# An attention and mixture-of-experts kernel on one core: five steps of blocks 2 to 4 change places in the order table

## The chip, the cores and the metric

The kernel runs on one core of a Trainium2 chip. The metric is device time in microseconds (us), the median of the runs; lower is better. The core's engines work side by side, each through its own instructions in a fixed order: TensorE (PE; PEld is its weight load), VectorE (DVE), ScalarE (ACT), GpSimd (POOL) and SyncE (SP), which issues most transfers.

## The reference

A gated linear attention runs over 768 steps for 4 x 8 heads of width 48; its output, laid out as 3072 tokens of 384 numbers, goes through a three-way maximum layer and then through a layer that sends each token to one of 8 experts.

```python
for t in range(S):
    state = alpha[:, :, t, :, None] * state + np.einsum('bhd,bhe->bhde', k[:, :, t], v[:, :, t])
    y[:, :, t] = np.einsum('bhd,bhde->bhe', q[:, :, t], state)
...
h = np.maximum(np.maximum(x @ w1, x @ w2), x @ w3)
return (h @ w_out).astype(np.float32)
...
e_idx = np.argmax(logits, axis=1)
...
h = np.maximum(x[mask] @ w1[e], 0.0)
ye = h @ w2[e]
out[mask] = gate_w[mask, None] * eom[mask, e, None] * ye
```

## The kernel before, in words

The 3072 tokens are eight blocks of 384, numbered 0 to 7. Blocks 2b and 2b+1 are the two halves of batch b. Each block passes through these steps:

- **Preparation of q and k** (DVE). `prep_z` runs a scan backwards over the decay factors into a tile `Z` (L196), `prep_k` multiplies k by it (L201), `prep_p` forms inverses and runs a forward scan over the same tile (L208 to L211), `prep_q` multiplies q by that (L215). Each is done once for either half b of the head pairs. There is one `Z`, so the four steps of one half end before those of the next begin. `check` and `check_pl` (ACT, L180 and L182) test the factors' range.
- **Attention by chunks.** `last` calls `attend`, which finishes one chunk (c, b) and begins the next: on PE transposes (L307), products with the state (L298), with the scores (L314) and with v (L320), new scores (L327); on DVE the state (L341, L343) and the masked scores A (L354); on ACT the state's decay (L346) and a copy of the result into `x32` (L351). The result of a block's last chunk is the last part of its x.
- **Split.** `split_x` cuts x into a high part (ACT, L368) and a low part (DVE, L369), three pieces each.
- **First layer.** `mm1` is called 18 times for a block (6 slices f, 3 matrices w). A call is a group of nine matmuls (L457) into one of three PSUM banks of the pool psM. ACT copies the group of w = 0 (`hm`, L461); DVE takes the maximum with those of w = 1 (L464) and w = 2 (L467); ACT and POOL then split the result (L478, L483). A bank is free again when it has been read.
- **Second layer.** `mm2` multiplies a tile of 128 tokens into `ops` (L493), and ACT copies the logits and the row out (L499, L500).
- **Routing** of a block. `route_a` finds the expert of each token and the running counts, eleven small DVE instructions (L528 to L544) with two exponentials on ACT (L532, L546); `route_b` forms ranks on PE (L551, L552, tile `rps`); `route_c` works the ranks out on DVE, beginning with the read of `rps` at L564; `route_d` forms the weights (L586 to L594).

For blocks 2 and up `ops` lies in the pool psO, and so does `rps` of `route_b` for all blocks but the last. That pool has one buffer, so the next user waits until the last reader of the one before is done:

```python
psO = pool("psO", bufs=1, space=PSUM)
...
free = i == NBLK - 1 and t == 1 or not general and (i == 0 or i == 1 and t != 1)
ops[t] = bank(psM, "M", "ops") if free else bank(psO, "O", "ops")
...
ps = rtmp["ps"] = bank(psO, "O", "rps") if i < NBLK - 1 else bank(C["psR"], "R", "rps")
```

The order of the work is a table written by hand. `on(t, f, ...)` notes a step with a place number t, `seq(t, dt, ...)` a row of steps that are dt apart; the steps are sorted by t and called in that order, and each engine works its instructions off in the order in which they were called. Numbers matter only by comparison: `mm1(i, f, w)` of blocks 2 and up has the number 18i + 3f + w, `mm2(2, 0)` has 54.9. The steps of the change have numbers between 30 and 54.

Of the kernel before, what the change touches and what calls it, by code (L numbers as in the profile page):

```python
# [88 lines left out]
def layers(tc, pool, wk, K, general, *args):  # L89
    with ExitStack() as ctx:  # L90
        _layers(ctx, tc, pool, wk, K, general, *args)


def _layers(ctx, tc, pool_, wk, K, general, qk, al, a0, v, vT, w123, wout, gates, ew1, ew2, out):
# [263 lines left out]
    def finish_x(i):  # L358
        for c in range(3):
            for h in range(2):  # L360
                (nc.sync if i < 2 else nc.scalar).dma_start(out=x32[i][64 * h + D:64 * h + 64, c],
                                                            in_=x32[i][64 * h + 16 * c:64 * h + 16 * c + 16, 3])
# [765 lines left out]
    def on(t, f, *a):  # L1128
        ev.append((t, len(ev), f, a))

    def seq(t, dt, *steps):

        for n, (f, *a) in enumerate(steps):
            on(t + n * dt, f, *a)
# [4 lines left out]
    if not general:  # L1139
        batches = [(c, b) for c in range(CPB) for b in (1, 0)]  # L1140

        def last(i, x, y=None):

            def f():
                attend(x and (i, *x), y and (i, *y))
                if x == (2, 1):
                    finish_x(i)
            return (f,)
# [57 lines left out]
        for (i, f), x in zip(order, steps):  # L1206
# [5 lines left out]
        lo, hi = range(3), range(3, 6)  # L1212
# [4 lines left out]
            (mm2, 0, 2, hi), (load_qkv, 3), (mm2, 1, 0, lo), last(2, (2, 1), (0, 0)), (check, 2, 0, 0),  # L1217
            (mm2, 1, 0, hi), (mm2, 1, 1, lo), last(2, (0, 0), (1, 0)), (check, 2, 0, 1), (load_a, 3, 0),
            (prep_z, 3, 1), (mm2, 1, 1, hi), last(2, (1, 0), (2, 0)), (prep_k, 3, 1),
            (mm2, 1, 2, lo), (check_pl, 3), (prep_p, 3, 1), last(2, (2, 0)), (split_x, 2), (mm2, 1, 2, hi), (prep_q, 3, 1),  # L1220
            (route_a, 0))
        seq(37.3, 0.9, (prep_z, 3, 0), (check, 3, 1, 0), (prep_k, 3, 0), (check, 3, 1, 1), (prep_p, 3, 0), (check, 3, 0, 0),
            (prep_q, 3, 0), (check, 3, 0, 1))
        seq(49.7, 0.6, (route_b, 0), (route_c, 0), (route_d, 0), (route_a, 1))
        seq(52.7, 0.6, (route_b, 1), (route_c, 1), (route_d, 1))
        on(42.9, load_a, 4, 1)
        on(45.1, load_a, 4, 0)

# [261 lines left out]
```

## Time and profile before

| what | value |
|---|---|
| median of 3 runs | 734.69 us (733.62 to 734.71) |
| the profiled execution's own time | 733.51 us |
| its span | 731.8 us |
| PE busy, share of the span | 699.3 us, 96% |
| DVE, ACT, POOL busy | 399.7, 290.3, 125.8 us |
| mean granted TensorE clock | 0.988 |

The span runs from the first to the last instruction. All starts below are microseconds from the span's start. An engine's idle time stands in square brackets before the instruction that ended it, with what released it. PEclk 1.00 is the clock's upper level (2.4 GHz), 0.50 the lower one (1.2 GHz). The changed steps lie between 147 and 211 us; blocks 2 to 7, and behind them the experts, follow.

### The profile page before, as it was taken

The numbers are of one execution on the slowest core, as the hardware profiler recorded it, in microseconds if no ns is written. First come the engines' busy times: TensorE is split into PE (matmuls) and PEld (weight loads), VectorE is DVE, ScalarE is ACT, GpSimd is POOL, SyncE is SP. The second block draws the span as 40 slices with busy tenths as digits, with TensorE's granted clock in tenths as the row PEclk, the third lists the DMA queues.
The fourth block names the chain that finished last, engine by engine and source line by source line (L and its number), as shares of the span: only waits on it lengthen the run. The fifth ranks groups of instructions, "written<-read, shape, count | busy, mean of one in ns | idle before, by whom it ended". The sixth has DMA issues, their size and how long they took to land.

```text
span 731.8 us, 14142 instructions
## 1 busy us (share of the span) xinstructions
PE 699.3 (96%) x5103; PEld 657.4 (90%) x5103; DVE 399.7 (55%) x951; ACT 290.3 (40%) x761; POOL 125.8 (17%) x136
## 2 busy tenths in 40 slices
PE   8999999999899999999999999989999999999992
PEld 7888999889799999998999999989879899999992
DVE  6868887376876736736324255664125254225451
ACT  4345533545543533524323214323224354334451
POOL 1000000001111111211111114042223233332320
PEclk9999999999999999999999999999999999999997
DMA  9906310651231510400000015016547342125430
GB/s 252 366 19 188 105 46 2 179 150 43 72 95 36 136 41 20 128 22 21 2 33 9 12 33 226 23 43 224 207 165 266 127 143 60 57 79 187 141 114 21
DMA packets 23069, 74.91 MB, mean 102 GB/s; under 512 B 7962, under 2 KB 12132, under 8 KB 19888
## 3 DMA queue, kind: packets, MB, share of 16 engines
q1 hardware_dynamic: 17424, 60.95, 25.4%
q0 software_dynamic: 4384, 11.72, 5.2%
q10 hardware_dynamic: 1152, 0.89, 0.5%
q8 instruction: 56, 0.92, 0.5%
q14 instruction: 53, 0.43, 0.2%
HBM read 100.67 MB, written 9.94 MB: 151 GB/s over the span
## 4 chain that ended last, share of the span: by engine, by line
PE 78%; DVE 9%; issue 4%; ACT 3%; DMA 3%; ACTq 1%; POOL 0%; SPq 0%; DVEq 0%; POOLq 0%
PE hps L457 25%; PE psM L990 13%; PE psP L1047 12%; PE ops L493 9%; PE sc L327 4%; PE y L314 3%; DMA out<-yo,sidx 2%; PE y L298 2%; PE psw L1122 1%; PE psM L982 1%; PE psP L982 1%; DVE Z L211 1%; PE XT L307 1%; PE psH L951 1%; DVE wu L414 1%
## 5 line engine op out<-in xcount | busy, mean ns | idle before, releaser
L990 PE MATMUL psM<-cx,w1H 128*128 128x256 f32 (+1 forms) x576 | 110.3, 290 | 3.2 <-DVE ch L997 3.2
L483 POOL TENSOR_TENSOR hL<-hm,hH 128x384 fp32r<-128x384 f32 x36 | 42.2, 1172 | 399.1 <-ACT hH L478 399.1
L457 PE MATMUL hps<-xH,wH 128*128 128x384 f32 x432 | 104.6, 349 | 1.5 <-ACT xH L368 1.3
L457 PE MATMUL hps<-xH,wL 128*128 128x384 f32 x432 | 99.1, 337 | 1.6 <-DVE wL L426 1.6
L1047 PE MATMUL psP<-w2H,ch 128*128 128x384 f32 x368 | 99.3, 341 | 1.0 <-issue 1.0
L457 PE MATMUL hps<-xL,wH 128*128 128x384 f32 x432 | 99.0, 336 | 0.0
L990 PEld LDWEIGHTS psM<-cx,w1H 128*128 128x128 f32 x576 | 90.9, 188 | 4.5 <-DVE ch L997 4.1
L997 DVE SCALAR_TENSOR_TENSOR ch<-psM,ch 128x256 fp32r<-128x256 f32 (+1 forms) x128 | 43.8, 371 | 91.0 <-ACT ch L994 83.4
L990 PE MATMUL psM<-cx,w1L 128*128 128x256 f32 (+1 forms) x288 | 83.2, 289 | 0.0
L457 PEld LDWEIGHTS hps<-xH,wH 128*128 128x128 f32 x432 | 74.7, 189 | 7.4 <-ACT xH L368 2.1
L457 PEld LDWEIGHTS hps<-xH,wL 128*128 128x128 f32 x432 | 77.4, 189 | 2.3 <-DVE wL L426 2.3
L457 PEld LDWEIGHTS hps<-xL,wH 128*128 128x128 f32 x432 | 77.7, 189 | 0.2 <-DVE xL L369 0.2
L1047 PEld LDWEIGHTS psP<-w2H,ch 128*128 128x128 f32 x368 | 66.8, 188 | 3.8 <-issue 3.1
L493 PE MATMUL ops<-wo,hH 128*128 128x400 f32 x258 | 68.4, 346 | 0.2
L464 DVE TENSOR_TENSOR hm<-hm,hps 128x384 f32<-128x384 f32 x48 | 26.4, 551 | 70.6 <-PE hps L457 65.1
L994 ACT ACTIVATE ch<-psM 128x256 fp32r<-128x256 f32 (+1 forms) x96 | 37.9, 401 | 61.0 <-PE psM L990 58.4
L1047 PE MATMUL psP<-w2L,ch 128*128 128x384 f32 x184 | 61.7, 335 | 0.1
L990 PEld LDWEIGHTS psM<-cx,w1L 128*128 128x128 f32 x288 | 54.5, 189 | 0.0
L478 ACT CAST hH<-hm 128x384 fp32r<-128x384 f32 x43 | 22.0, 512 | 81.6 <-DVE hm L467 77.8
L1010 POOL DMA_INDIRECT out<-yo,sidx x27 | 28.9, 1072 | 128.7 <-ACT yo L1058 30.2
L493 PEld LDWEIGHTS ops<-wo,hH 128*128 128x128 f32 x258 | 47.0, 188 | 1.3 <-ACT hH L478 0.5
L493 PE MATMUL ops<-wo,hL 128*128 128x400 f32 x129 | 44.5, 345 | 0.5 <-POOL hL L483 0.5
(263 smaller groups left out, 1122.1 us busy)
## 6 DMA issues: line engine op xcount, KB each, us to landing
s1a<-in_ew SPq DMA_DIRECT2D x12, 1536.0 KB
s2a<-in_ew SPq DMA_DIRECT2D x12, 1536.0 KB
s1b<-in_ew SPq DMA_DIRECT2D x8, 1536.0 KB
s2b<-in_ew SPq DMA_DIRECT2D x8, 1536.0 KB
ws<-in_w SPq DMA_DIRECT2D x6, 1152.0 KB
at<-in_al SPq DMA_DIRECT2D x16, 336.9 KB
vt<-in_v SPq DMA_DIRECT2D x8, 576.0 KB
x2d<-xs SPq DMA_DIRECT2D x24, 192.0 KB
```

Of the source, the lines that this page charges most:

```text
L314: mm(y[64 * h:64 * h + D, g], vt[i][:, c, hh * D:(hh + 1) * D], A[:, h, g], start=(first and g == 0 and not on_pe), stop=True, skip_group_ ...
L327: mm(sc[:, h, g * L:(g + 1) * L], kt[ni][r, 2 * nb + g, ncs], qt[ni][r, 2 * nb + g, ncs], start=True, stop=True)
L457: mm(ps, slab(a, f)[:, w, k], b[i][:, k], start=(n == 0), stop=(n == 8))
L464: nc.vector.tensor_max(m, m, ps)
L478: nc.scalar.copy(hH[i, f], m)
L483: (nc.gpsimd if not general and i > 1 else nc.vector).tensor_sub(hL[i, f], hps["m"], hH[i, f].bitcast(F32))
L493: mm(ps[:, :DM + NG], a[i, f][:, ts_], wo[f // 3][:, b, f % 3], start=(f + n == 0), stop=(f + n == 7))
L990: mm(ps, w[:, k, f * 128:(f + 1) * 128], x[:, k, :n], start=(k + m == 0), stop=(k + m == 4))
L994: nc.scalar.activation(chid(0, f, slice(0, n)), ps, AF.Relu)
L997: nc.vector.scalar_tensor_tensor(C["h"][f // 4][:, f % 4, to:to + b - a], ps[:, a:b], 0.0, chid(0, f, slice(a, b)).bitcast(F32), op0=ALU.m ...
L1010: nc.gpsimd.indirect_dma_start(out=out[:, :], out_offset=bass.IndirectOffsetOnAxis(ap=sidx[:p, c:c + 1], axis=0), in_=y[:p], in_offset=Non ...
L1047: mm(ps[:, :DM], chid(x, f, slice(128 * t, 128 * t + 128)), w[:, f], start=(f + n == 0), stop=(f == NE - 1 and n == 2))
```

## The change

Only the table's numbers and the places of steps in it change; every instruction is kept.

```diff
@@ -1217,12 +1217,13 @@
             (mm2, 0, 2, hi), (load_qkv, 3), (mm2, 1, 0, lo), last(2, (2, 1), (0, 0)), (check, 2, 0, 0),
             (mm2, 1, 0, hi), (mm2, 1, 1, lo), last(2, (0, 0), (1, 0)), (check, 2, 0, 1), (load_a, 3, 0),
             (prep_z, 3, 1), (mm2, 1, 1, hi), last(2, (1, 0), (2, 0)), (prep_k, 3, 1),
-            (mm2, 1, 2, lo), (check_pl, 3), (prep_p, 3, 1), last(2, (2, 0)), (split_x, 2), (mm2, 1, 2, hi), (prep_q, 3, 1),
+            (mm2, 1, 2, lo), (check_pl, 3), last(2, (2, 0)), (split_x, 2), (mm2, 1, 2, hi), (prep_p, 3, 1), (prep_q, 3, 1),
             (route_a, 0))
         seq(37.3, 0.9, (prep_z, 3, 0), (check, 3, 1, 0), (prep_k, 3, 0), (check, 3, 1, 1), (prep_p, 3, 0), (check, 3, 0, 0),
-            (prep_q, 3, 0), (check, 3, 0, 1))
-        seq(49.7, 0.6, (route_b, 0), (route_c, 0), (route_d, 0), (route_a, 1))
-        seq(52.7, 0.6, (route_b, 1), (route_c, 1), (route_d, 1))
+            (check, 3, 0, 1), (prep_q, 3, 0))
+        seq(49.7, 0.6, (route_b, 0), (route_c, 0), (route_d, 0))
+        on(51.9, route_a, 1)
+        seq(53.2, 0.4, (route_b, 1), (route_c, 1), (route_d, 1))
         on(42.9, load_a, 4, 1)
         on(45.1, load_a, 4, 0)
 
```

`prep_p(3, 1)` moves behind the last chunk of block 2, `split_x(2)` and `mm2(1, 2, hi)`. `prep_q(3, 0)` and `check(3, 0, 1)` change places. `route_a(1)` moves from 51.5 to 51.9, `route_b(1)` from 52.7 to 53.2, `route_c(1)` from 53.3 to 53.6 and `route_d(1)` from 53.9 to 54.0.

On DVE, at the split of block 2's x (Z, d and pl belong to the preparation of block 3, xL is the split's low part):

```order
 L201 TENSOR_TENSOR kt<-kt,Z 112x768
+L343 TENSOR_TENSOR state<-state,y 48x2x48 x2
+L369 TENSOR_TENSOR xL<-x_1347,xH 128x384 x3
 L208 TENSOR_SCALAR d_131<-Z 112x2x3
 L209 TENSOR_TENSOR pl<-pl,Z 112x6
 L210 RECIPROCAL d_131<-d_131 112x2x3
 L211 SCALAR_TENSOR_TENSOR Z<-at,d_131 112x769
-L343 TENSOR_TENSOR state<-state,y 48x2x48 x2
-L369 TENSOR_TENSOR xL<-x_1347,xH 128x384 x3
 L215 TENSOR_TENSOR qt<-qt,Z 112x768
```

The last state and the split's subtractions stand ahead of the inverses and the forward scan of the preparation now; the multiplication of q stays behind both.

On DVE, at block 1's routing, the changed order from the last instruction of `route_a(1)` to the first two of `route_c(1)` (L564 reads `rps`; Z and kt belong to block 5, state and A to block 4):

```order
+L544 TENSOR_REDUCE z<-rv 128x3
+L369 TENSOR_TENSOR xL<-x_1825,xH 128x384 x3
+L464 TENSOR_TENSOR hm<-hm,hps 128x384
+L467 TENSOR_TENSOR hm<-hm,hps 128x384
+L196 SCALAR_TENSOR_TENSOR Z<-at,dz 112x769
+L201 TENSOR_TENSOR kt<-kt,Z 112x768
+L341 COPY state<-y 48x2x48 x2
+L354 TENSOR_TENSOR A<-sc,mask 128x512
 L564 TENSOR_TENSOR rd<-rps,oh 128x24
 L568 TENSOR_REDUCE ri<-rd 128x3
```

The scan, the product with k, the state and the mask (L196, L201, L341, L354) stand ahead of L564 now; they stood behind `route_c(1)`. The whole of `route_a(1)` also moved behind the preparation L208 to L215 of block 4, ahead of which it stood.

On PE, at the same place (hps is the last group of nine of block 2, `mm1(2, 5, 2)`; XT begins a chunk of block 4):

```order
+L457 MATMUL hps<-xH,wH_885 128x384 x3
+L457 MATMUL hps<-xL,wH_885 128x384 x3
+L457 MATMUL hps<-xH,wL_886 128x384 x3
 L551 LDWEIGHTS ut
 L551 MATMUL rps<-oh,ut 128x24
 L552 LDWEIGHTS ones
 L552 MATMUL rps<-oc,ones 128x24
-L457 MATMUL hps<-xH,wH_885 128x384 x3
-L457 MATMUL hps<-xL,wH_885 128x384 x3
-L457 MATMUL hps<-xH,wL_886 128x384 x3
 L307 MATMUL XT<-ident,kt 128x112 x2
```

The two matmuls into `rps` moved behind one group of nine and stand directly ahead of the chunk. POOL's and SP's orders are the same as before.

## Rows read from the trace of the kernel before

**Rows 1.** The page: busy time of each engine, then the chain that ended last.

```profile
PE 699.3 (96%) x5103; PEld 657.4 (90%) x5103; DVE 399.7 (55%) x951; ACT 290.3 (40%) x761; POOL 125.8 (17%) x136
...
PE 78%; DVE 9%; issue 4%; ACT 3%; DMA 3%; ACTq 1%; POOL 0%; SPq 0%; DVEq 0%; POOLq 0%
```

**Rows 2.** Timeline, PE waits: start us, us, engine line op out<-in, [idle before <- releaser].

```profile
152.51 1.27 PE L457 MATMUL hps<-xH,wH 128*128 128x384 f32 x3 [1.33 <-ACT xH L368]
...
197.39 0.19 PE L551 MATMUL rps<-oh,ut 128*128 128x24 bf16 x1 [0.71 <-DVE oh L538]
...
201.47 0.71 PE L327 MATMUL sc<-qt,kt 48*128 48x128 f32 x8 [0.89 <-DVE qt L215]
```

**Rows 3.** Timeline around the split of block 2's x, DVE, ACT and PE.

```profile
149.00 0.35 PE L320 MATMUL y<-vt,kn 128*48 128x48 f32 x8
...
150.59 0.49 DVE L343 TENSOR_TENSOR state<-state,y 48x96 f32<-48x96 f32 x2
...
151.95 1.34 ACT L368 CAST xH<-x 128x384 fp32r<-128x384 f32 x3
...
152.49 1.49 DVE L369 TENSOR_TENSOR xL<-x,xH 128x384 fp32r<-128x384 f32 x3 [1.41 <-ACT xH L368]
...
156.60 0.18 DVE L544 TENSOR_REDUCE z<-rv 128x3 f32<-128x24 f32 x1
...
156.93 0.46 ACT L461 COPY hm<-hps 128x384 f32<-128x384 f32 x1
...
158.17 0.56 DVE L464 TENSOR_TENSOR hm<-hm,hps 128x384 f32<-128x384 f32 x1 [1.39 <-PE hps L457]
```

**Rows 4.** Timeline, PE: starts of block 2's first groups, and the transpose after six.

```profile
154.98 1.17 PE L457 MATMUL hps<-xH,wH 128*128 128x384 f32 x3
...
157.86 0.80 PE L457 MATMUL hps<-xH,wH 128*128 128x384 f32 x3
...
159.53 0.68 PE L457 MATMUL hps<-xH,wH 128*128 128x384 f32 x3
...
164.22 0.36 PE L307 MATMUL XT<-ident,kt 112*128 112x112 f32 x2
```

**Rows 5.** Two stretches: us, busy (x instructions) of PE PEld DVE ACT POOL, PEclk, DMA.

```profile
154.00:158.00 4.00, 4.00 (x15) 3.96 (x15) 2.43 (x11) 0.79 (x3) 0.00 (x0) 0.58 0.63 120
...
480.00:484.00 4.00, 2.82 (x24) 2.82 (x25) 2.77 (x5) 2.55 (x6) 2.29 (x2) 1.00 0.16 53
```

**Rows 6.** Timeline around block 1's routing: DVE, and PE weight loads (PEld).

```profile
196.30 0.17 DVE L528 TENSOR_REDUCE mx<-lg 128x3 f32<-128x24 f32 x1
...
198.05 0.18 DVE L544 TENSOR_REDUCE z<-rv 128x3 f32<-128x24 f32 x1
...
198.15 0.16 DVE L208 TENSOR_SCALAR d<-Z 112x6 f32<-112x6 f32 x1
...
201.24 1.49 DVE L369 TENSOR_TENSOR xL<-x,xH 128x384 fp32r<-128x384 f32 x3
...
202.65 0.54 DVE L464 TENSOR_TENSOR hm<-hm,hps 128x384 f32<-128x384 f32 x1
...
203.77 0.17 DVE L564 TENSOR_TENSOR rd<-rps,oh 128x24 f32<-128x24 f32 x1
...
204.06 0.30 PEld L493 LDWEIGHTS ops<-wo,hH 128*128 128x128 f32 x2 [0.40 <-PE hps L457]
...
205.65 1.75 DVE L196 TENSOR_TENSOR_SCAN Z<-at,dz 112x769 f32<-112x769 f32 x1
...
207.43 0.96 DVE L201 TENSOR_TENSOR kt<-kt,Z 112x768 f32<-112x768 f32 x1
...
209.47 0.17 DVE L586 TENSOR_REDUCE se<-rex 128x3 f32<-128x24 f32 x1
...
209.66 0.42 PEld L314 LDWEIGHTS y<-A,vt 128*48 128x48 f32 x8 [0.51 <-ACT x L351]
```

**Rows 7.** Timeline, DVE: the product with k while POOL runs.

```profile
225.43 1.59 DVE L201 TENSOR_TENSOR kt<-kt,Z 112x768 f32<-112x768 f32 x1
```

## The prediction

> **What bounds the kernel now.** I read the page first: PE is busy 96% of the span and the chain that ended last is 78% PE [rows 1]. So a step that moves on another engine is worth only what PE waits for at that place. I then listed the waits of PE itself on the timeline between 125 and 250 us, where the changed steps lie, and read who released each. Three of them touch moved steps [rows 2]: 1.33 us until 152.51, for the high part of block 2's x; 0.71 us until 197.39, for `oh` of `route_a(1)`; 0.89 us until 201.47, for a product with q. Together they are 2.93 us, which is all that the change could give back without the clock. Outside this stretch nothing is moved, and PE has so few gaps behind it that I take a shift gained or lost here to last to the end.
>
> The reader is to see that each of these waits ends with a chain on DVE or ACT that the table ordered badly for PE, and also that DVE's rows from 196.30 to 209.47 have no idle time before them [rows 6]: there an instruction that is called earlier always makes another one late.
>
> **Part A, the split of block 2's x.** DVE ran the inverses and the forward scan of a preparation ahead of the last state, though PE had finished its matmul at 149.00 + 0.35 = 149.35; the state began only at 150.59 [rows 3]. Without `prep_p` in front it can begin about 0.1 us after PE, at 149.45, so 1.14 us earlier. The copy, the high part and the low part follow the state at fixed distances (1.36 us to the high part, 0.54 from there to the low part [rows 3]), on ACT without other work between. PE's first group of block 2 moves from 152.51 to 151.37. The matmuls ahead of it end at 152.51 - 1.33 = 151.18 [rows 2], so 0.2 us of the wait is left.
>
> What was moved is late next. DVE is through with the low part at 151.35 + 1.41 = 152.76 (1.41: from its start to the next instruction, 201.24 to 202.65 [rows 6]). Then come `prep_p` and `prep_q`, 198.15 to 201.24 = 3.09 us [rows 6], and `route_a(0)`, whose last reduction begins 1.75 us after its first (196.30 to 198.05 [rows 6]): 152.76 + 3.09 + 1.75 = 157.60, against 156.60 before [rows 3]. ACT can't pass its exponential on that result, and the copy of the first group stands behind it, 0.33 us later and 0.46 long [rows 3]: it ends at 158.39, against 157.39. PE has three banks. Its first group takes 154.98 - 152.51 = 2.47 us, as before, since it is paced by the pieces of the split; two more take 1.56 each (three groups lie between 159.53 and 164.22, 4.69 / 3 [rows 4]). They end at 151.37 + 2.47 + 3.13 = 156.97. The fourth needs the bank that ACT frees at 158.39, so PE waits some 1.5 us and goes on at 158.5, and reaches the transpose 4.69 us later, at 163.2 instead of 164.22 [rows 4]. DVE, which had 1.39 us of idle time at 158.17 [rows 3], can follow. **Part A gains 1.0 us**, not the 1.33 us of the wait and not the clock's share either, which is in this number: before, the second group took 157.86 - 154.98 = 2.88 us [rows 4], because the clock was at its lower level (mean 0.58 from 154 to 158 [rows 5]) after the wait of 1.33 us and a first group with gaps in it.
>
> That the new wait of 1.5 us leaves the clock up is my choice; the nearest row for it is 480 to 484 us, where PE was busy 2.82 of 4 us and the clock stayed at 1.00 [rows 5]. The nearest row against it is 154 to 158. So A lies between a loss of 0.4 (a group at 2.88 instead of 1.56 costs 1.3, and 1.0 - 1.3 - 0.1 for the rest of the stretch) and a gain of 2.0 (if PE finds the bank free).
>
> [...]
>
> **`prep_q(3, 0)` behind a check.** I cost it at nothing. Its user, the scores of block 3's fourth chunk, comes three chunks later; the check on ACT moves ahead of the next chunk's copies, on an engine with 40% load [rows 1]; one transfer of alpha for block 4 starts earlier into an empty stretch.
>
> **Part B, block 1's routing.** All times are those of before; they would start 1.0 us earlier. DVE begins `route_a(1)` at 196.30 and the preparation of block 4 at 198.15 [rows 6]. In the new order the preparation comes first: 196.30 + 3.09 = 199.39, then `route_a(1)`, whose last reduction begins at 201.14. The product with q is done sooner, so the 0.89 us go. But PE now has the group of nine first, ends it near 196.68 + 1.56 = 198.2, and then waits for `oh` until about 200.5: a wait of some 2.2 us takes the place of 0.71.
>
> ACT casts block 3's high part only behind the exponential of `route_a(1)`: 201.14 + 0.33 = 201.47, and DVE's low part follows 0.54 us later at 202.01 (201.24 before). The first maximum (L464) comes at 202.01 + 1.41 = 203.42 instead of 202.65 [rows 6].
>
> Now the step that decides. `route_c(1)`'s first instruction, L564, reads `rps` and so frees psO's only bank for `mm2(2, 0)`. Before, L564 began at 203.77 and PE's weight load for `ops` at 204.06, 0.29 us later [rows 6]: PE was hardly held. In the new order four instructions stand ahead of L564: scan, product with k, state, mask, which took from 205.65 to 209.47 = 3.82 us [rows 6]. They begin where L564 would have, 203.42 + (203.77 - 202.65) = 204.54, and end at 208.36. POOL's subtraction for the last hidden slice starts during that scan; where it did so at 225.43, the product with k took 1.59 us instead of the 0.96 at 207.43 [rows 6, 7]. I add these 0.63. L564 begins at 208.99, `mm2(2, 0)` at 209.28. PE, done with block 3's first group by about 204.6, waits 4.7 us. The start of `mm2(2, 0)` moves by 209.28 - 204.06 = 5.2 us. Given back: the next chunk waited 0.51 us for a copy behind the state [rows 6], and this state is early now. **Part B costs 4.7 us**; between 4.1 (POOL does not meet the product) and 5.3 (nothing given back).
>
> **The clock behind it.** Two waits, of some 2.2 and 4.7 us, are longer than the one before the fall in rows 4 and 5, so I take the clock to fall. A fall after the first wait costs nothing, for it slows a group that ends in the second wait. One after the second falls on dense matmuls and costs what rows 4 show: 2.88 - 1.56 = 1.3 and a tenth in the next group (1.67), 1.4 us. Bounds: 0 and 2.8 (two such stretches).
>
> **The sum.** -1.0 + 4.7 + 1.4 = +5.1 us. The profiled execution took 733.51 us, 1.18 less than the median of 734.69 and within the runs' spread. On its own time the sum gives 738.6; the runs to be compared are medians, so I forecast 734.69 + 5.1 = **739.8 us**.
>
> **Rivals.**
> - *PE is not held at `mm2(2, 0)`* (the other side). The place is psO's bank, the price is the 4.7 us. It decides at about 204.6: if L564 has read by then, part B is 0.6 us of a later first group less 0.1 and 0.51 given back, nothing. With A alone the time is 733.7, and 732.7 if A gives its upper 2.0. For it: in the trace of before PE was held there by 0.1 us at most. Against it: one bank, DVE full, and 3.8 us of work in front. Chance 0.04, half of it past 0.2% faster.
> - *The clock does not fall behind the long wait, or falls and is hidden*: +3.7, 738.4 us. Chance 0.18.
> - [...] Chance 0.16.
> - *The forecast*, one fall behind the long wait: 0.62.
>
> **How the numbers follow.** A measurement of this kernel tells some 0.2%, 1.5 us, from no change. The second, third and fourth case all lie over that: together 0.96, of which I put 0.01 to no change for a part B much smaller than worked out, so slower 0.95; same is that 0.01 and half of the first rival, 0.03; faster its other half, 0.02. The range takes in the second and third case and the bounds of A (a gain of 2.0) and B: low 734.69 - 2.0 + 4.1 + 0 = 736.8; high 741.2 + 0.6 for B + 0.7 for half of a second slow stretch = 742.5.
>
> **What would show it.** In the profile of the changed kernel PE's wait ahead of block 2's first group is under 0.4 us, and a new wait of 1 to 2 us stands two groups later, released by ACT's copy L461. The matmuls into `rps` of block 1 follow the last group of block 2 after about 2 us of idle PE, and ahead of `mm2(2, 0)` stands 4 to 5 us, ended by DVE L564. PEclk falls once in the 4 us behind it and no longer at 154 to 158. The forecast is wrong if PE's idle time at `mm2(2, 0)` is under 1 us, or if it is long and the time is still not longer, which would mean that a later stretch had slack.

## The result and the profile after

| | before | changed |
|---|---|---|
| median | 734.15 us (733.24 to 734.71, 4 runs) | 741.00 us (740.23 to 741.05, 4 runs) |
| ratio, 95% interval | | 1.0095 (1.0081 to 1.0109) |
| profiled execution: own time, span | 733.51, 731.8 us | 741.02, 739.2 us |
| mean granted TensorE clock | 0.988 | 0.988 |

The kernel became 6.85 us slower; 5.1 us were forecast, and 741.0 lies in the range. The page of the changed kernel shows the same work on the engines as [rows 1], 7.4 us more span, and in its group list one new wait of several us:

```profile
PE 700.6 (95%) x5103; PEld 657.8 (89%) x5103; DVE 399.6 (54%) x951; ACT 290.9 (39%) x761; POOL 126.0 (17%) x136
...
L493 PE MATMUL ops<-wo,hH 128*128 128x400 f32 x258 | 70.0, 353 | 4.9 <-DVE rd L564 4.8
```

The 258 matmuls of this form of `mm2` waited 4.9 us in all, 4.8 of them for `rd` of L564. PE's waits between 148 and 215 us on the timeline (start, duration, instruction, in brackets the wait ahead of it and its releaser) answer to [rows 2]:

```profile
150.16 1.27 PE L457 MATMUL hps<-xH,wH 128*128 128x384 f32 x3 [0.24 <-ACT xH L368]
...
157.33 0.79 PE L457 MATMUL hps<-xH,wH 128*128 128x384 f32 x3 [1.54 <-ACT hm L461]
...
166.99 0.75 PE L298 MATMUL y<-qt,state 112*112 112x128 f32 x4 [0.53 <-ACT state L346]
...
199.25 0.19 PE L551 MATMUL rps<-oh,ut 128*128 128x24 bf16 x1 [2.24 <-DVE oh L538]
...
208.04 1.01 PE L493 MATMUL ops<-wo,hH 128*128 128x400 f32 x2 [4.77 <-DVE rd L564]
```

The reader is to see five things: 0.24 us in place of 1.33 ahead of block 2; a new 1.54 us ahead of that block's fourth group, ended by ACT's copy L461; a new 0.53 us at the first chunk behind; 2.24 us in place of 0.71 for `oh`; and 4.77 us ahead of `mm2(2, 0)`, ended by L564. The wait of 0.89 us for a product with q is gone. The timeline of DVE, and of POOL beside it, answers to [rows 6]:

```profile
203.30 1.75 DVE L196 TENSOR_TENSOR_SCAN Z<-at,dz 112x769 f32<-112x769 f32 x1
...
204.00 1.83 POOL L483 TENSOR_TENSOR hL<-hm,hH 128x384 fp32r<-128x384 f32 x1 [10.21 <-ACT hH L478]
...
205.08 1.57 DVE L201 TENSOR_TENSOR kt<-kt,Z 112x768 f32<-112x768 f32 x1
...
206.57 0.51 DVE L341 COPY state<-y 48x96 f32<-48x96 f32 x2
...
207.12 0.69 DVE L354 TENSOR_TENSOR A<-sc,mask 128x512 f32<-128x512 f32 x1
...
207.73 0.17 DVE L564 TENSOR_TENSOR rd<-rps,oh 128x24 f32<-128x24 f32 x1
```

DVE works without idle time from 203.30 on: scan, product with k, state and mask, and only at 207.73 the read that frees psO's bank. PE's last group had ended near 203.3. Stretches of this kernel (us, busy time of PE, PEld, DVE, ACT, POOL, then PEclk):

```profile
153.00:157.00 4.00, 2.78 (x17) 2.46 (x15) 3.28 (x12) 0.52 (x3) 0.00 (x0) 1.00 0.89 224
...
204.00:208.00 4.00, 0.00 (x0) 0.00 (x0) 3.89 (x7) 1.01 (x4) 1.83 (x1) 0.72 0.25 79
...
208.00:212.00 4.00, 3.96 (x12) 3.99 (x13) 1.25 (x10) 1.29 (x3) 0.00 (x0) 0.50 0.05 0
```

PE is idle from 204 to 208, and from 208 to 212 it runs `mm2` at PEclk 0.50; from 153 to 157, where [rows 5] show 0.58 a little later, the clock stays at 1.00. `mm2(2, 0)` takes 5.41 us (208.04 to 213.45, the start of the next group), against 3.34 in the profile of before (204.09 to 207.43).

I followed the difference by the starts of the same PE instruction in both traces. At 70 us, ahead of every moved step, the changed kernel was 1.10 us early: in the profile of before the clock was at a mean of 0.57 from 11 to 15 us, here at 1.00. Such an offset is taken out below, for every kernel. Net of it the change stands at -0.1 us at 187 us, +5.05 at the start of `mm2(2, 0)`, +7.1 at its end, +6.7 behind the next chunk, and still +6.7 at 400 us. So what the change does, it does between 150 and 216 us.

### The profile page after: what moved, and what is told of

It is laid out like the page before. It is cut to its first block, busy times and chain, and to the rows that moved or that the text cites. A ratio compares the mean times of both kernels' runs of the same rounds, so it can differ in the third digit from the quotient of the medians.

```text
span 739.2 us, 14141 instructions
## 1 busy us (share of the span) xinstructions
PE 700.6 (95%) x5103; PEld 657.8 (89%) x5103; DVE 399.6 (54%) x951; ACT 290.9 (39%) x761; POOL 126.0 (17%) x136
## 5 line engine op out<-in xcount | busy, mean ns | idle before, releaser
L493 PE MATMUL ops<-wo,hH 128*128 128x400 f32 x258 | 70.0, 353 | 4.9 <-DVE rd L564 4.8
L464 DVE TENSOR_TENSOR hm<-hm,hps 128x384 f32<-128x384 f32 x48 | 26.4, 551 | 76.3 <-PE hps L457 68.3
L478 ACT CAST hH<-hm 128x384 fp32r<-128x384 f32 x43 | 22.0, 512 | 79.7 <-DVE hm L467 75.8
```

Source lines behind the costliest of these rows:

```text
L464: nc.vector.tensor_max(m, m, ps)
L478: nc.scalar.copy(hH[i, f], m)
L493: mm(ps[:, :DM + NG], a[i, f][:, ts_], wo[f // 3][:, b, f % 3], start=(f + n == 0), stop=(f + n == 7))
```

## The experiments

Ratios go to the kernel before on the same chip: 733.07 us (23 runs) for the first four, 733.36 us (23 runs) for the next four. "Net" is the shift of PE's starts at 400 us against the first profile of before, less the offset at 70 us.

| kernel | median, us | ratio, 95% interval | net, us |
|---|---|---|---|
| e1: the split alone | 733.38 | 1.0005 (0.9989 to 1.0020) | 0.0 |
| e2: the routing alone | 739.52 | 1.0105 (1.0084 to 1.0125) | +6.2 |
| e3: the change, L564 ahead of the scan | 734.10 | 1.0015 (1.0001 to 1.0029) | +1.2 |
| e4: the change, `rps` in psM | 736.75 | 1.0055 (1.0034 to 1.0077) | +3.7 |
| e5: the split, without `route_a(0)` behind it | 731.82 | 0.9981 (0.9967 to 0.9995) | -2.6 |
| e6: the kernel before, routing of block 1 late | 731.41 | 0.9973 (0.9956 to 0.9989) | -3.8 |
| e7: e5 and e6 | 727.98 | 0.9923 (0.9902 to 0.9943) | -5.1 |
| e8: e7, a product with q one chunk later | 727.68 | 0.9923 (0.9898 to 0.9949) | -5.6 |

**e1, the split alone.** Of the change only `prep_p(3, 1)` is moved:

```diff
-            (mm2, 1, 2, lo), (check_pl, 3), (prep_p, 3, 1), last(2, (2, 0)), (split_x, 2), (mm2, 1, 2, hi), (prep_q, 3, 1),
+            (mm2, 1, 2, lo), (check_pl, 3), last(2, (2, 0)), (split_x, 2), (mm2, 1, 2, hi), (prep_p, 3, 1), (prep_q, 3, 1),
```

> The kernel before with part A alone (prep_p(3, 1) behind the split and the second layer's last matmuls). Theory 1: the 1.0 us that PE has gained at block 2's first transpose is given back within 5 us, because VectorE's maxima and ScalarE's copies, casts and checks of these groups now follow one another without a gap; the sum of part A is -0.1 us, 734.0. Theory 2 (the forecast's term): the gain of 1.0 us lasts, 733.1. Both: no stretch at the lower clock at 154 us.

Measured: no difference, 1.0005. PE's waits in the stretch:

```profile
151.74 1.27 PE L457 MATMUL hps<-xH,wH 128*128 128x384 f32 x3 [0.24 <-ACT xH L368]
...
158.91 0.79 PE L457 MATMUL hps<-xH,wH 128*128 128x384 f32 x3 [1.54 <-ACT hm L461]
...
168.58 0.75 PE L298 MATMUL y<-qt,state 112*112 112x128 f32 x4 [0.54 <-ACT state L346]
```

PE is ahead of before until the transpose behind six groups, by 0.8 us net, and has 0.1 of it left at the first chunk behind. ACT's and DVE's timeline of this kernel shows the chain:

```profile
158.39 0.46 ACT L461 COPY hm<-hps 128x384 f32<-128x384 f32 x1
...
161.59 0.52 ACT L478 CAST hH<-hm 128x384 fp32r<-128x384 f32 x1 [2.73 <-DVE hm L467]
...
162.01 0.93 ACT L182 ACTIVATE am<-at,b_lo 112x762 bf16<-112x762 f32 x1
...
162.94 0.46 ACT L461 COPY hm<-hps 128x384 f32<-128x384 f32 x1
...
163.43 0.56 DVE L464 TENSOR_TENSOR hm<-hm,hps 128x384 f32<-128x384 f32 x1 [1.00 <-ACT hm L461]
...
168.14 0.67 ACT L346 ACTIVATE state<-state,pl 112x112 f32<-112x112 f32 x2
```

The late copy L461 makes the maxima late, the second of them stands behind a scan on DVE, ACT's cast L478 waits 2.73 us for it, the range check L182 and the next copy follow the cast, and DVE waits 1.00 us for that copy. The state's decay L346 comes last in this row, and PE waits 0.54 us for it. In the profile of before the same maximum L464 was released by PE's matmuls, not by ACT's copy:

```profile
162.92 0.55 DVE L464 TENSOR_TENSOR hm<-hm,hps 128x384 f32<-128x384 f32 x1 [1.21 <-PE hps L457]
```

**e2, the routing alone.** Of the change only the three lines of block 1's routing.

```diff
-        seq(49.7, 0.6, (route_b, 0), (route_c, 0), (route_d, 0), (route_a, 1))
-        seq(52.7, 0.6, (route_b, 1), (route_c, 1), (route_d, 1))
+        seq(49.7, 0.6, (route_b, 0), (route_c, 0), (route_d, 0))
+        on(51.9, route_a, 1)
+        seq(53.2, 0.4, (route_b, 1), (route_c, 1), (route_d, 1))
```

> The kernel before with the four routing steps of block 1 moved as in the change, and nothing else. Theory 1: the whole loss stands here, +6.9 us (741.0), since part A is worth nothing: a wait of 2.2 us ahead of the matmuls into rps, one of 4.8 us ahead of mm2(2, 0), and 2 us of slow clock behind that. Theory 2 (part A lasts with 1.0 us): +7.9 us, 742.

Measured: 1.0105, the whole loss of the change. PE's waits, and two stretches:

```profile
199.44 0.19 PE L551 MATMUL rps<-oh,ut 128*128 128x24 bf16 x1 [2.26 <-DVE oh L538]
...
208.24 1.01 PE L493 MATMUL ops<-wo,hH 128*128 128x400 f32 x2 [3.29 <-DVE rd L564]
```

```profile
201.00:205.00 4.00, 3.96 (x17) 3.41 (x17) 3.90 (x6) 3.22 (x10) 0.80 (x1) 0.57 0.87 280
...
208.00:212.00 4.00, 3.76 (x13) 3.77 (x14) 1.42 (x12) 1.46 (x4) 0.00 (x0) 0.59 0.05 0
```

Here the clock fell behind the first wait too (0.57 from 201 to 205 us). The slower group ended inside the time in which the bank was held anyway, so the wait for L564 is 3.29 us instead of 4.77 and the start of `mm2(2, 0)`, net, is as late as in the change: +5.2 us. `mm2(2, 0)` then takes 4.74 us, 1.40 more than before.

**e3, the read ahead of the scan.** The change with `route_b(1)` and `route_c(1)` close behind each other:

```diff
-        seq(53.2, 0.4, (route_b, 1), (route_c, 1), (route_d, 1))
+        seq(53.2, 0.05, (route_b, 1), (route_c, 1))
+        on(54.0, route_d, 1)
```

> The change, but route_c(1) is called at 53.25, directly behind route_b(1) and ahead of block 5's prep_zk, so that L564 stands ahead of the scan on VectorE again; all else as in the change. Theory 1 (PE waits for the read of rps behind scan, product, state and mask): the wait ahead of mm2(2, 0) falls from 4.8 us to under 0.5, the clock stays up, and the time is 734 to 735.5. Theory 2 (the 2.2 us wait and the later split of block 3 cost it): 738 or more.

Measured: 1.0015, which is 1.0 us by the medians in place of 6.85. On DVE and PE:

```profile
200.83 0.19 PE L551 MATMUL rps<-oh,ut 128*128 128x24 bf16 x1 [2.26 <-DVE oh L538]
...
204.88 0.18 DVE L564 TENSOR_TENSOR rd<-rps,oh 128x24 f32<-128x24 f32 x1
...
206.14 0.52 PE L493 MATMUL ops<-wo,hH 128*128 128x400 f32 x2
...
206.76 1.75 DVE L196 TENSOR_TENSOR_SCAN Z<-at,dz 112x769 f32<-112x769 f32 x1
```

L564 runs at 204.88, before PE has ended the group, and `mm2` starts without a wait and takes 3.27 us. The seven small instructions cost 1.9 us of DVE ahead of the scan and nobody on PE. Of the waits of the change only those for `oh` and `oc` (2.26 and 0.20 us) are left; the clock fell behind them here (mean 0.57 from 202 to 206 us), which theory 1 had not expected, and the net is +1.2.

**e4, another bank.** The change with `rps` of block 1 in the pool psM, so that `mm2(2, 0)` need not wait for its reader:

```diff
-        ps = rtmp["ps"] = bank(psO, "O", "rps") if i < NBLK - 1 else bank(C["psR"], "R", "rps")
+        ps = rtmp["ps"] = bank(psM, "M", "rps") if i == 1 and not general else bank(psO, "O", "rps") if i < NBLK - 1 else bank(C["psR"], "R", "rps")
```

> The change, every order as in it, but rps of block 1 lies in a bank of psM instead of psO. VectorE reads it as late as in the change. Theory 1 (the wait is for psO's one bank): mm2(2, 0) doesn't wait for L564, no fall of the clock, 734 to 735. Theory 2 (VectorE's backlog itself holds PE, by masks, states or maxima): a wait of some 4 us turns up within the next 6 us of PE work, 738 or more. The first wait of 2.2 us is there under both, and shows by itself whether it makes the clock fall.

Measured: 1.0055, between the two theories. The order on DVE is that of the change, and PE doesn't wait at `mm2(2, 0)`:

```profile
199.52 0.19 PE L551 MATMUL rps<-oh,ut 128*128 128x24 bf16 x1 [2.27 <-DVE oh L538]
...
203.14 1.30 PE L457 MATMUL hps<-xH,wH 128*128 128x384 f32 x3 [1.40 <-DVE hm L464]
```

```profile
201.00:205.00 4.00, 2.60 (x18) 2.42 (x15) 3.86 (x6) 3.30 (x11) 0.72 (x1) 0.57 0.97 306
...
205.00:209.00 4.00, 4.00 (x15) 3.98 (x14) 3.78 (x12) 1.56 (x4) 1.12 (x1) 0.58 0.03 8
```

So it was the bank, as T1 says. But `rps` holds one of psM's three banks now, and block 3's first group waits 1.40 us for the maximum L464 of the group before; behind the two waits the clock is at 0.57 and 0.58 over eight microseconds. T1's time left both out.

**e5, the split without `route_a(0)` behind it.** e1, and `route_a(0)` called at 44.5, in the middle of block 2:

```diff
-            (mm2, 1, 2, lo), (check_pl, 3), (prep_p, 3, 1), last(2, (2, 0)), (split_x, 2), (mm2, 1, 2, hi), (prep_q, 3, 1),
-            (route_a, 0))
+            (mm2, 1, 2, lo), (check_pl, 3), last(2, (2, 0)), (split_x, 2), (mm2, 1, 2, hi), (prep_p, 3, 1), (prep_q, 3, 1),
+            )
+        on(44.5, route_a, 0)
```

> The split moved ahead of the preparation as in the change, the rest of block 2 to 4 as before, and block 0's route_a(0) taken out of the work behind the split: it is called at 44.5, in the middle of block 2's groups. T1 (the 1.0 us was given back because route_a(0), with DVE's reductions and ACT's exponentials, makes ACT's copy of the first group late and so DVE's maxima): the wait of 1.54 us for the copy L461 shrinks to under 0.5 us, no fall of the clock between 150 and 160 us, and the time is 1.0 to 2.5 us under the kernel before. T2 (the stretch is bound by the preparation and the range check, whatever stands behind them): a wait of over 1 us for L461 stays, and the time is within 0.5 us of the kernel before.

Measured: 0.9981, 1.4 us faster. ACT copies the first group as soon as PE has it, DVE takes the maximum at 154.93, and PE waits for nothing from there to the chunk:

```profile
150.32 1.27 PE L457 MATMUL hps<-xH,wH 128*128 128x384 f32 x3 [0.24 <-ACT xH L368]
...
152.85 0.48 ACT L461 COPY hm<-hps 128x384 f32<-128x384 f32 x1 [1.18 <-PE hps L457]
...
154.93 0.56 DVE L464 TENSOR_TENSOR hm<-hm,hps 128x384 f32<-128x384 f32 x1
...
164.64 0.74 PE L298 MATMUL y<-qt,state 112*112 112x128 f32 x4
```

So T1: the small DVE instructions of `route_a(0)` (ten of them in the trace, not eleven) and its two exponentials, not the preparation, made the gain of part A go again. The net of -2.6 us is more than the 1.4 us of the times. Of it, 1.6 came at the groups behind 152 us, where the clock fell in the first profile of before and stayed up here. In how many executions of before it falls is not known; e6 and e9 below come back to it.

**e6, the routing late.** The kernel before with block 1's routing behind the second `mm2` of block 2:

```diff
-        seq(49.7, 0.6, (route_b, 0), (route_c, 0), (route_d, 0), (route_a, 1))
-        seq(52.7, 0.6, (route_b, 1), (route_c, 1), (route_d, 1))
+        seq(49.7, 0.6, (route_b, 0), (route_c, 0), (route_d, 0))
+        on(57.5, route_a, 1)
+        on(58.4, route_b, 1)
+        on(58.45, route_c, 1)
+        on(58.7, route_d, 1)
```

> The kernel before with block 1's routing moved as a whole to 57.5 (route_a) and 58.4 to 58.7 (route_b to route_d), between the second and the third mm2 of block 2, where DVE had idle time. T1 (the routing costs what stands in DVE's full stretch; where DVE is idle it costs nothing): the waits of 0.71, 0.20 and 0.89 us near 197 to 202 us go, none over 0.5 us takes their place, the time is 1.5 to 2.5 us under the kernel before. T2 (the one bank of psO makes any place between two mm2 cost a wait): the old waits go, but the third mm2 of block 2 waits 1 us or more for L564, and the time is within 0.5 us of the kernel before or above it.

Measured: 0.9973, 2.0 us faster.

```profile
151.70 1.27 PE L457 MATMUL hps<-xH,wH 128*128 128x384 f32 x3 [1.33 <-ACT xH L368]
...
197.69 0.72 PE L327 MATMUL sc<-qt,kt 48*128 48x128 f32 x8 [0.45 <-DVE qt L215]
...
212.63 0.17 DVE L528 TENSOR_REDUCE mx<-lg 128x3 f32<-128x24 f32 x1
...
214.62 0.19 PE L551 MATMUL rps<-oh,ut 128*128 128x24 bf16 x1
...
215.36 0.18 DVE L564 TENSOR_TENSOR rd<-rps,oh 128x24 f32<-128x24 f32 x1
...
218.54 0.52 PE L493 MATMUL ops<-wo,hH 128*128 128x400 f32 x2
```

```profile
153.00:157.00 4.00, 4.00 (x24) 3.78 (x23) 3.01 (x13) 0.84 (x4) 0.00 (x0) 1.00 0.59 106
```

The routing takes DVE's time from 212.63 to 218.2, and neither `rps` nor the next `mm2` has a wait ahead of it (0.45 us for a product with q are left, at 197.69): L564 reads 3.2 us before the bank is wanted. T2 falls: the bank costs nothing where the read comes before PE's next use. Of the net -3.8 us, -1.7 came at the groups behind 152 us, where nothing is moved: there the clock stayed at 1.00 in this profile, behind the same wait of 1.33 us. Of these, -1.3 were left at 187 us; the other -2.5 came behind 195 us, with the routing.

**e7 and e8, both, and one wait more.** e7 has the edits of e5 and e6. e8 also calls `prep_pq(4, 1)` at 48.05, one chunk later.

> The edits of e5 and e6 in one kernel. T1: what PE no longer waits for adds up, so the difference to the kernel before is that of e5 plus that of e6, some 3 to 4.5 us less. T2 (the waits of one stretch are given back in the next): no more than the larger of the two.

> As e7, with the multiplication of q for half 1 of block 4 called at 48.05, one chunk later, so that it no longer stands between the state and the mask before the chunk at 186 us. T1 (the wait of 0.9 us there for ACT's copy into x32 comes from DVE's preparation in front): that wait goes and the time is 0.5 to 1 us under e7. T2: the same wait comes at the next chunk, the time is that of e7.

Measured: both 0.9923, 5.6 us faster than the kernel before, and so some 12.5 us faster than the changed one, which is 6.85 slower than before (the two were not run side by side). The stretch in e8, from 146 to 246 us:

```profile
146.00:246.00 100.00, 98.82 (x780) 91.59 (x779) 78.88 (x175) 49.39 (x145) 15.57 (x11) 1.00 0.35 95
```

PE is busy 98.82 of 100 us at a clock of 1.00. e7's gain is at least the sum of e5's and e6's (0.19% and 0.27%), so T1 holds, and its 3 to 4.5 us were too few; why the two together give more than their sum is not shown. In e8's trace the wait of 0.93 us at 186 us is gone and the net is 0.6 us better than e7's; the times cannot tell the two apart.

**e9, the kernel before again.** Unchanged, one run of 733.54 us.

> The kernel before, unchanged, profiled a second time. In e6, which calls the same steps up to 190 us, the clock did not fall behind the same wait of 1.33 us ahead of block 2. T1 (the fall at 154 us in the first profile of before is one of several outcomes of the same program and no fixed part of its time): PEclk from 153 to 158 us is 1.00, and PE reaches the first chunk of block 3 some 1.5 us earlier, counted from its start at 70 us, than in the first profile. T2 (it belongs to the program): the clock falls there again and the second group takes 2.9 us.

T1 missed: the clock fell again behind the wait of 1.32 us, to a mean of 0.57:

```profile
153.00:157.00 4.00, 4.00 (x15) 3.77 (x15) 2.64 (x12) 0.87 (x4) 0.00 (x0) 0.57 0.59 123
```

Of four profiles with this wait ahead of block 2 (before, e2, e6, e9) three show the fall and one, e6, does not. Both profiles of the kernel before have it; e6 calls the same steps up to there and shows that it need not come. Four profiles do not tell how often it does.

## Why the prediction was right, and which term was off

**What bounds, and where.** Right: the moved steps, which belong to the preparation of block 3 and the routing of block 1, act on PE between 150 and 216 us alone, and the shift is the same at 400 us.

**Part B.** Forecast: `mm2(2, 0)` starts 5.2 us later for a wait of 4.7 us, and with 0.51 given back it costs 4.7. Measured: 5.18 later against PE's shift ahead of it (+3.95, from -1.23), a wait of 4.77, and 0.41 given back, so 4.77. The steps are the forecast's: the wait for `oh` was to be some 2.2 us and was 2.24; four instructions before L564; the product with k was to take 1.59 us beside POOL and took 1.57. POOL's subtraction ends at 205.83, 0.75 us after that product's start. The Trainium skill, page "SBUF — State Buffer", section "SBUF: two separate sides", says that a DVE instruction with two inputs in SBUF and a GpSimd instruction that reads SBUF lock a shared pair of ports, and that the one that comes second is blocked until the other ends; by that rule the estimate is 0.75 + 0.96 = 1.71 us, which the measured 1.57 comes near and does not quite reach. In e3, where POOL's subtraction had ended before (205.59 + 1.03 = 206.62), the product with k at 208.54 took 0.96 us. e2 shows the whole term alone: net +6.2 with its clock, where 4.7 + 1.4 were forecast. e3 and e4 show the mechanism from two sides: with the read early, or the bank another one, the wait is gone.

**The clock.** One fall behind the long wait, forecast at 1.4 us. In e2 it cost 1.40. In the change it cost 2.07 us (5.41 - 3.34): the clock was down through the four microseconds behind the wait, not for one group. The term was 0.7 too small, within the bound of 2.8 that the forecast gave.

**Part A is the term that was mis-sized.** The forecast was a gain of 1.0 us that lasts. At the transpose behind six groups it was there: 164.22 [rows 4] became 162.12, that is 2.10 earlier, 1.0 net of the offset. The wait of 0.24 us and the 1.54 us for L461 were as worked out. Then 0.9 us went again, and at 187 us -0.1 was left. The failing step is the sentence that DVE, with its 1.39 us of idle time, "can follow". That idle time lay in front of one maximum; the work behind it is a chain over two engines (scan, maximum, cast, range check, copy), and DVE was made to wait inside it. The rows of this chain stand under e1; in the changed kernel they are the same, 1.58 us earlier, with the same 1.00 us ahead of the maximum L464. I had carried the delay through ACT's first copy only. e1 measures the term alone as no gain (1.0005), and e5, which takes `route_a(0)` out of this chain, gets 1.4 us.

**The sum.** -0.13 + 4.77 + 2.07 = +6.7 us against -1.0 + 4.7 + 1.4 = +5.1; the medians gave +6.85. Two terms were off by 0.9 and 0.7, both on the same side.

**The rivals.** That PE is not held at `mm2(2, 0)` is refuted by the wait of 4.77 us. That the clock does not fall, or that its fall is hidden, is refuted for the second wait; for the first one the forecast's "costs nothing" was seen in e2. That the clock falls in part A too did not come: PEclk is 1.00 from 153 to 162 us in the change, behind a wait of 1.54 us, and from 157 to 165 us in e1, e3 and e4, behind 1.52 to 1.54 us. So no run shows the 1.4 us that make 741.2 us out of the forecast and stand in the range's upper end; that the median of 741.0 lies so near is chance, for what was missing in the sum is the lost gain of part A and the longer fall behind `mm2(2, 0)`. The Trainium skill, page "TensorE: Matmul & The Clock Gate", section "HAM oscillation — how this bites in real kernels", tells of a wait between bursts of matmuls that is long enough to drop the array to half rate, so that the next burst starts cold. The traces agree for the waits ahead of `mm2(2, 0)`: behind 4.77 us in the change and 3.29 us in e2, PEclk is 0.50 and 0.59 from 208 to 212 us.

## What to carry to other kernels

Where a pool has one buffer, the place of its reader in the reader's engine decides when the next writer starts: keep short reads that free a bank ahead of long work, or put the whole job where that engine idles (e6). Before moving long work ahead of such a read, write down what then stands in front of it, and who waits. And when a delay is carried forward, follow it around the whole chain over the engines until it meets idle time on each: idle time in front of one instruction is not slack of the chain.

## What the runs showed of the hardware that was not expected

- The same wait does not always bring the same clock. Behind 1.32 to 1.33 us ahead of block 2 it fell in three profiles of four. Behind 2.24 to 2.27 us for `oh` it fell in e2, e3 and e4 (0.57 to 0.62 from 201 to 205 us) and stayed at 1.00 in the change. So the forecast's terms for the clock are likely values, not fixed ones, and one profile does not tell which of its slow stretches come back.
- In the change and in five of the nine other kernels (e5 to e9) PE waits about 0.5 us near 500 us for a branch in DVE's instructions or for an unnamed cause, such as:

```profile
506.30 0.39 PE L990 MATMUL psM<-cx,w1L 128*128 128x256 f32 x1 [0.57 <-DVEq L1394]
```

The unchanged kernel of e9 has it (0.52 us), the first profile of before has not; why is open, and it is no part of the change.
